# Sliding-window attention and a residual MLP: the same tasks in another written-out order

## The chip, the cores and the metric

The kernel runs on one core of a Trainium2 chip. Its time is the device time of one execution in microseconds (us). A profile is one further execution recorded by the hardware profiler; its span runs from the first to the last instruction of the core and is somewhat shorter than the time.

The core has these engines: TensorE (PE: matmuls and transposes; its weight loads are listed as PEld), VectorE (DVE), ScalarE (ACT), GpSimd (POOL) and SyncE (SP), which only issues transfers here. Transfers can be issued by SP and ACT (the profile's queue q1 is SP's, q10 is ACT's) and by GpSimd (queue q0, "software_dynamic"). Sixteen DMA engines carry all of them.

## The reference

Attention with a window of 128 keys and 4 sink keys, over 4 batches, 8 heads, 768 positions and 64 dimensions, and then a residual MLP with a mixing step over the positions. All inputs and the output are float32.

```python
def _attn_ref(q, k, v, n_sink, window):          # q, k, v: (4, 8, 768, 64)
    scores = scale * np.matmul(q, k.transpose(0, 1, 3, 2))
    keep = is_sink | in_window
    scores = np.where(keep, scores, -1000000000.0)
    a = softmax(scores)                          # written out in the original
    return np.matmul(a, v)

def _moe_ref(x, alpha1, beta1, w_tok, alpha2, beta2, w_ch1, w_ch2, lam):
    a1 = alpha1 * x + beta1                      # x: (4, 768, 512)
    tok = np.einsum('ts,bsd->btd', w_tok, a1)
    u = x + lam * tok
    a2 = alpha2 * u + beta2
    ch = np.maximum(a2 @ w_ch1, 0.0) @ w_ch2     # w_ch1: 512 x 2048
    return u + lam * ch
```

## The kernel before

**A list of tasks.** The kernel's body is written as 1143 tasks. Each is a Python function that issues one to some twenty instructions; it names the tasks whose results it needs and the buffers it uses. Nothing is issued while the tasks are collected. At the end one call writes them out by four tables of literals:

```python
plan.emit(ORDER, ENGINES, HOMES, IDLES)
```

ORDER is the sequence of task numbers in which the instructions are issued. Since each engine works off its instructions in the order in which they were issued, it fixes the stream of every engine and of every DMA queue. ENGINES gives for each task one digit: 0 ACT, 1 DVE, 2 TensorE, 3 GpSimd, 4 SP. HOMES says which slot of its kind each buffer takes (8 slots for q and k rows, `nat`; 4 for staged weights, `wst`; 2 for `hT`; and so on). IDLES lists filler matmuls on a tile `warm` of zeros (L148) that are put ahead of a task: `(73, 0, 65)` means 65 of them before task 73. The priorities and costs in the task functions play no part on the chip: there only true dependences of data and buffers, and the order of the queues, act.

**Stages.** Batch 0 starts with loads. `load_qk` (L397) brings q or k of a pair of heads (384 KB) through SP or ACT; for the later pairs of batch 0 (L390) GpSimd's queue brings them and converts to float16 on the way. `load_v0` (L424) brings v in blocks, `load_wtok` (L435) rows of w_tok. `trans` transposes q and k on TensorE (L507 for the pair that was cast on the core, L504 for those cast on the way), and the results are copied to `qkT` (L157). Then come the masked scores per block of 128 positions (bias and q k products, L612, L617, L678, L681), exponentials (L639, L686), the product with v (`pv`, L718), the division (L743, L744), and the multiplication with lam-alpha1 into `xh`, in halves of 256 columns on GpSimd in batch 0 (L753). `cast_wtok` casts and transposes w_tok (L809). `tok` (L849) is the mixing over positions, after which u is formed (L856) and cast (L155, L157).

For the channel MLP u is transposed (`uTp`, L890) and taken through the affine alpha2, beta2 (L873 on ACT). `mlp1` computes h for one block `fi` of 128 of the 2048 channels and 384 positions (four matmuls, L929), followed by a relu on ACT (L935) or DVE (L937). Block `fi` needs quarter `fi // 4` of w_ch1. The second product (L1046 and L1114) gives the result, which is added and stored (L1065, L1128). The batches follow each other; the attention of the next batch is woven into the MLP of the one before.

**Weights.** `load_w1` (L448) brings one quarter of w_ch1 (512 columns, 1 MB of float32 read) through GpSimd's queue, which converts it into the float16 tile `w1f`. `load_w2` (L444) brings pieces of w_ch2 into `wst`, from where `cast_w2` casts them. `lam_b` (L1235) is lam spread over the partitions.

**Gates.** A gate is a transfer of eight elements out of `w1f` through SP:

```python
def gate(i):
    add(-3000, {SP: 790}, lambda e: nc.sync.dma_start(
        gates[0:1, 8 * i : 8 * i + 8], w1f[0:1, 0, i * 512 : i * 512 + 8]), [done["w1", i]],
        lands=(1, 20))
```

It reads what quarter i writes, so SP waits there until that quarter has landed, and everything that stands behind it on SP's queue waits with it. There are gates for quarters 1, 2 and 3.

**The order before, around the change.** SP starts with row 0 of w_tok, q and k of pair 0, then v and the rest of w_tok, then a piece of w_ch2, lam, another piece of w_ch2, the gate of quarter 1, and only then loads for batch 1 and more of w_ch2, with the gates of 2 and 3 further on. GpSimd starts with k of pair 1, a small constant (`sel`), q of pair 1, another load, masks, another load, `bm`, and the identity `iden` (L326), which every transpose needs. After the first half of `xh` (L753) it issues the quarters 0, 1, 2, 3 of w_ch1 one after another, and then goes on with the halves. TensorE starts with 65 fillers, the transposes of w_tok 0 (L809), 12 fillers, the transposes of q and k of pair 0 (L507), those of k of pair 1 (L504), fillers, and scores. Its first h tasks are those of fi 1, 11, 8, 13, 12, 14; then come the `uTp` of the other half.

Of the kernel before, what the change touches and what calls it, by code (L numbers as in the profile page):

```python
# [77 lines left out]
def kernel(  # L78
# [119 lines left out]
    for r in range(NR):  # L198
# [18 lines left out]
        26, 6, 9, 7, 10, 5, 11, 8, 18, 15, 72, 19, 1, 12, 3, 0, 4, 2, 22, 14, 73, 74, 45, 48, 46,  # L217
        17, 39, 49, 47, 53, 13, 40, 50, 41, 90, 95, 43, 91, 51, 54, 103, 52, 16, 44, 61, 104, 42,
        96, 109, 100, 62, 107, 110, 63, 55, 28, 108, 92, 56, 101, 21, 68, 65, 59, 93, 20, 69, 97,
        102, 111, 94, 24, 98, 57, 60, 30, 112, 105, 23, 58, 99, 113, 128, 106, 114, 116, 25, 131,  # L220
        135, 78, 115, 64, 27, 138, 31, 32, 117, 132, 29, 129, 136, 33, 122, 66, 125, 34, 123, 137,
        119, 139, 126, 35, 79, 70, 120, 140, 124, 84, 71, 80, 133, 130, 141, 67, 146, 85, 134, 121,
        147, 144, 75, 118, 158, 86, 154, 148, 159, 145, 142, 87, 149, 150, 155, 160, 143, 76, 88,
        151, 156, 81, 77, 166, 152, 162, 167, 89, 127, 82, 163, 213, 83, 168, 209, 164, 165, 214,
        210, 153, 217, 179, 211, 178, 157, 197, 229, 36, 212, 215, 218, 185, 216, 226, 230, 219,
        176, 161, 177, 220, 169, 223, 222, 232, 225, 224, 221, 227, 237, 233, 279, 238, 234, 228,
        273, 280, 182, 171, 204, 291, 274, 175, 289, 292, 200, 231, 293, 290, 246, 294, 295, 199,
        384, 241, 248, 188, 186, 257, 296, 247, 172, 243, 277, 174, 181, 242, 259, 258, 187, 170,
        278, 267, 37, 260, 271, 358, 268, 198, 285, 349, 272, 381, 301, 286, 366, 351, 303, 302,
        189, 297, 378, 173, 304, 281, 180, 352, 203, 249, 190, 282, 298, 379, 250, 287, 380, 192,  # L230
        353, 385, 288, 206, 283, 386, 369, 375, 367, 265, 284, 368, 202, 370, 266, 363, 376, 371,
        253, 377, 201, 299, 254, 372, 364, 183, 382, 191, 300, 373, 615, 365, 275, 374, 383, 357,
        261, 276, 408, 262, 387, 263, 184, 409, 205, 195, 239, 411, 264, 410, 395, 269, 396, 240,
        397, 270, 196, 388, 614, 621, 235, 412, 400, 194, 244, 398, 236, 401, 255, 617, 251, 245,
        256, 389, 390, 399, 252, 311, 359, 207, 193, 391, 424, 616, 335, 425, 393, 341, 426, 392,
        336, 648, 427, 634, 413, 394, 312, 636, 414, 428, 419, 404, 420, 415, 360, 405, 313, 429,
        208, 422, 337, 416, 361, 441, 421, 622, 402, 314, 423, 442, 626, 403, 305, 638, 315, 406,
        430, 640, 316, 435, 431, 306, 641, 355, 436, 443, 619, 437, 338, 649, 618, 438, 362, 317,
        432, 637, 407, 307, 433, 345, 444, 339, 439, 635, 318, 445, 450, 434, 639, 644, 319, 451,
        628, 452, 620, 440, 308, 645, 340, 453, 417, 446, 323, 447, 418, 320, 309, 448, 324, 321,  # L240
        658, 322, 329, 449, 642, 659, 454, 325, 625, 643, 330, 646, 347, 455, 326, 623, 343, 647,
        464, 344, 456, 465, 348, 466, 460, 457, 467, 650, 327, 458, 331, 461, 629, 459, 472, 462,
        632, 463, 653, 356, 651, 656, 627, 332, 38, 654, 480, 333, 342, 624, 652, 473, 310, 476,
        468, 471, 470, 469, 481, 474, 488, 885, 477, 475, 482, 492, 655, 490, 493, 350, 483, 478,
        514, 491, 516, 489, 657, 479, 515, 660, 517, 630, 882, 665, 518, 663, 354, 328, 666, 502,
        880, 661, 664, 498, 879, 519, 508, 499, 346, 503, 678, 662, 512, 509, 679, 504, 513, 487,
        484, 671, 485, 676, 486, 506, 677, 877, 548, 505, 672, 680, 507, 526, 549, 546, 527, 631,
        334, 522, 674, 681, 528, 547, 907, 523, 534, 903, 529, 633, 682, 675, 878, 542, 683, 535,
        890, 689, 543, 550, 685, 684, 690, 510, 551, 494, 511, 673, 667, 544, 495, 668, 891, 496,
        686, 545, 901, 687, 669, 497, 693, 888, 688, 883, 530, 694, 670, 700, 531, 524, 897, 701,  # L250
        698, 500, 691, 525, 696, 699, 552, 501, 697, 704, 553, 558, 695, 705, 904, 692, 562, 559,
        706, 909, 887, 707, 563, 564, 898, 708, 702, 566, 565, 910, 715, 703, 567, 532, 716, 889,
        713, 533, 709, 714, 896, 520, 710, 556, 717, 521, 538, 557, 537, 540, 539, 536, 560, 541,
        899, 718, 921, 572, 922, 881, 711, 574, 884, 573, 576, 712, 561, 719, 902, 577, 575, 555,
        727, 720, 569, 908, 721, 580, 728, 578, 722, 581, 729, 554, 723, 905, 730, 568, 739, 724,
        579, 725, 592, 570, 911, 726, 582, 740, 593, 588, 912, 583, 595, 584, 571, 906, 743, 589,
        731, 585, 900, 590, 732, 605, 744, 587, 733, 596, 606, 734, 607, 611, 594, 597, 602, 745,
        612, 586, 613, 599, 895, 603, 591, 757, 765, 600, 758, 601, 759, 766, 741, 771, 760, 742,
        916, 772, 751, 917, 746, 773, 752, 913, 761, 919, 774, 886, 767, 918, 604, 762, 763, 598,
        768, 777, 764, 779, 920, 923, 780, 914, 755, 915, 778, 608, 756, 926, 930, 735, 609, 931,  # L260
        924, 927, 781, 736, 925, 775, 782, 737, 928, 753, 929, 893, 738, 934, 754, 892, 769, 935,
        932, 610, 941, 770, 819, 776, 942, 894, 939, 820, 821, 940, 937, 936, 823, 749, 822, 945,
        748, 824, 938, 747, 827, 933, 948, 950, 750, 952, 943, 951, 825, 953, 787, 828, 944, 807,
        788, 797, 826, 808, 949, 946, 829, 798, 801, 954, 830, 791, 802, 956, 947, 792, 783, 955,
        957, 963, 961, 784, 789, 958, 962, 811, 790, 964, 959, 785, 812, 965, 805, 786, 795, 806,
        960, 967, 796, 799, 793, 968, 966, 970, 972, 794, 813, 971, 969, 815, 973, 814, 809, 800,
        816, 803, 810, 974, 978, 804, 976, 979, 837, 975, 977, 835, 838, 980, 841, 836, 839, 842,
        818, 843, 840, 845, 981, 832, 982, 846, 817, 986, 844, 831, 990, 987, 983, 988, 847, 991,
        984, 851, 833, 992, 1002, 993, 834, 848, 855, 852, 985, 849, 1003, 859, 856, 1004, 989,
        1006, 850, 860, 1005, 853, 998, 1007, 1008, 868, 999, 857, 1009, 997, 865, 995, 858, 862,  # L270
# [35 lines left out]
    )  # L306
    IDLES = (
        (73, 0, 65), (46, 0, 12), (49, 1, 1), (90, 3, 10), (61, 3, 2), (109, 3, 3), (92, 3, 1),
        (166, 1, 4), (162, 0, 1),
    )  # L310
    W1_SINCE = 20000.0

# [1010 lines left out]
```

The softmax here doesn't subtract the row's maximum and nothing guards it: scores larger than these inputs give would overflow.

## Time and profile before

| what | value |
|---|---|
| time, median of 3 runs | 258.25 us (256.22 to 258.77) |
| span of the profiled execution | 254.3 us |
| mean granted TensorE clock | 0.997 |
| TensorE busy | 245.6 us (97%) |
| VectorE busy | 190.7 us (75%) |
| ScalarE busy | 133.2 us (52%) |
| GpSimd busy | 103.2 us (41%) |
| quarter of w_ch1, issue to landing | 9.6 / 15.4 / 20.2 us (min / median / max) |
| q or k through GpSimd's queue (L390) | 6.7 / 7.7 / 8.3 us |
| DMA moved | 38.79 MB, 153 GB/s over the span |

The profiled execution has no time of its own beside its span; the three timed runs lie 1.9 to 4.5 us above that span. Busy time counts an engine's instructions, fillers included. Where a row names what an engine waited for, it is the one of several things that came last by the profile.

### The profile page before, as it was taken

How to read it: one execution, taken by the hardware profiler on the slowest of the kernel's cores; microseconds unless marked ns; L12 is line 12 of the kernel's file. 1: busy time of each engine (PE TensorE's matmuls, PEld its weight loads, DVE VectorE, ACT ScalarE, POOL GpSimd, SP SyncE). 2: the span in 40 equal slices, each digit the busy share in tenths (PEclk: the TensorE clock that was granted, in tenths of full speed). 3: DMA queues.
4: the chain of work that ended last, by engine and by line, in shares of the span. 5: the costliest groups of instructions: out<-in, count | busy, mean ns of one | idle time of the engine just before them, and what ended most of it. 6: DMA issues, size and time to landing. Idle time of an engine off the chain costs nothing.

```text
span 254.3 us, 5499 instructions
## 1 busy us (share of the span) xinstructions
PE 245.6 (97%) x2167; PEld 159.9 (63%) x2167; DVE 190.7 (75%) x402; ACT 133.2 (52%) x219; POOL 103.2 (41%) x124
## 2 busy tenths in 40 slices
PE   7799997999999999999999999999999999999993
PEld 7554644666555544566687686667667676667882
DVE  5688986767888874978879995578778983228892
ACT  2599913879977034787833434566660235543000
POOL 8318845876455527515782040065662120000010
PEclk9999999999999999999999999999999999999998
DMA  6999999899999999998484764520000140100327
GB/s 182 205 215 266 272 269 316 246 377 300 221 158 233 234 208 156 195 249 180 110 170 107 128 122 138 144 65 0 3 0 3 30 84 13 41 0 3 117 73 268
DMA packets 86129, 38.79 MB, mean 153 GB/s; under 512 B 73540, under 2 KB 80460, under 8 KB 86104
## 3 DMA queue, kind: packets, MB, share of 16 engines
q1 hardware_dynamic: 66576, 28.06, 47.3%
q10 hardware_dynamic: 15784, 7.11, 11.8%
q0 software_dynamic: 3744, 3.28, 8.0%
q8 instruction: 17, 0.28, 0.4%
q14 instruction: 8, 0.07, 0.1%
HBM read 29.91 MB, written 6.29 MB: 142 GB/s over the span
## 4 chain that ended last, share of the span: by engine, by line
PE 84%; DMA 11%; DVE 2%; POOL 1%; SPq 0%; issue 0%
PE h L929 32%; PE P L1046 22%; PE tok L849 9%; PE ch L1114 8%; DMA w1f<-in_moe_w_ch_dram 8%; PE pv L718 3%; PE S L617 3%; DMA nat<-in_k_dram 3%; PE tp L507 1%; POOL w1f L448 1%; PE tp L504 1%; DVE qkT L157 1%; DVE E L696 1%; PE pv L711 1%; PE pv L604 1%; PE idle L148 0%
## 5 line engine op out<-in xcount | busy, mean ns | idle before, releaser
L929 PE MATMUL h<-uT,w1f 128*128 128x384 f16 x512 | 89.8, 326 | 1.5 <-DMA w1f<-in_moe_w_ch_dram 1.5
L929 PEld LDWEIGHTS <-w1f 128*128 128x128 f16 x512 | 48.2, 98 | 32.7 <-DMA w1f<-in_moe_w_ch_dram 1.9
L935 ACT ACTIVATE hT<-h 128x384 f16<-128x384 f32 x77 | 37.0, 491 | 39.5 <-PE h L929 39.3
L937 DVE TENSOR_SCALAR hT<-h 128x384 f16<-128x384 f32 x51 | 27.8, 555 | 23.4 <-PE h L929 22.8
L1046 PEld LDWEIGHTS <-hT 128*128 128x128 f16 x408 | 39.5, 98 | 6.7 <-issue 0.2
L639 ACT ACTIVATE E<-S 128x1024 f16<-128x1024 f32 (+1 forms) x39 | 38.1, 1001 | 7.6 <-PE S L617 6.3
L762 POOL TENSOR_TENSOR tm<-x,la_b 128x512 f32<-128x512 f32 x18 | 24.3, 1353 | 24.2 <-DVE x L744 12.3
L849 PE MATMUL tok<-xh,wtokT 128*128 128x512 f16 x144 | 33.0, 379 | 0.0
L1059 DVE TENSOR_TENSOR x<-x,P 128x256 f32<-128x256 f32 x45 | 18.3, 419 | 11.3 <-PE P L1046 10.2
L1046 PE MATMUL P<-w2f,hT 128*128 128x256 f16 x216 | 26.5, 273 | 0.0
L849 PEld LDWEIGHTS <-wtokT 128*128 128x128 f16 x144 | 13.9, 98 | 15.0
L1114 PE MATMUL ch<-w2f,hT 128*128 128x512 f16 x96 | 23.2, 379 | 0.0
L1046 PE MATMUL P<-w2s,hT 128*128 128x256 f16 x192 | 23.1, 273 | 0.0
L1082 POOL TENSOR_TENSOR x<-x,pt 128x256 f32<-128x256 f32 x4 | 3.4, 854 | 47.5 <-DVE pt L1077 47.5
L155 ACT CAST u<-x 128x512 f16<-128x512 f32 x15 | 9.2, 615 | 24.9 <-DVE x L856 24.3
L744 DVE TENSOR_TENSOR x<-pv,rec 128x256 f32<-128x256 f32 x48 | 20.4, 425 | 1.7
L155 ACT CAST n<-nat 128x768 f16<-128x768 f32 x21 | 16.9, 828 | 8.9 <-DVE x L1125 6.4
L718 PEld LDWEIGHTS <-E 128*128 128x128 f16 x328 | 14.8, 98 | 5.1 <-issue 1.1
L856 DVE TENSOR_TENSOR x<-x,tok 128x512 f32<-128x512 f32 x24 | 16.0, 683 | 2.3 <-PE tok L849 2.3
L718 PE MATMUL pv<-vfs,E 128*128 128x65 f16 x328 | 17.7, 194 | 0.0
L579 POOL TENSOR_SCALAR_AFFINE_SELECT E<-E 128x512 f16<-128x512 f16 x12 | 7.5, 648 | 20.6 <-ACT E L639 20.6
L743 DVE RECIPROCAL rec<-pv 128x4 f32<-128x4 f32 x48 | 8.6, 179 | 7.2 <-PE pv L718 6.9
(134 smaller groups left out, 340.6 us busy)
## 6 DMA issues: line engine op xcount, KB each, us to landing
wst_w<-in_moe_w_ch_dram SPq DMA_DIRECT2D x8, 512.0 KB, 8.2
nat<-in_q_dram SPq DMA_DIRECT2D x10, 384.0 KB, 3.9
vnat<-in_v_dram SPq DMA_DIRECT2D x14, 256.0 KB, 5.7
nat<-in_k_dram SPq DMA_DIRECT2D x8, 384.0 KB, 7.2
out_dram<-x SPq DMA_DIRECT2D x11, 256.0 KB, 3.1
out_dram<-x ACTq DMA_DIRECT2D x10, 256.0 KB, 3.7
wtn<-in_moe_w_tok_dram SPq DMA_DIRECT2D x6, 384.0 KB, 4.1
w1f<-in_moe_w_ch_dram POOLq DMA_DIRECT2D x4, 512.0 KB, 15.4
```

The costliest lines, as they stand in the source:

```text
L155: nc.scalar.copy(o, i)
L639: nc.scalar.activation(eT.t, pS.t[:, :, 0 : n * w].rearrange("p e (i w) -> p e i w", i=n), AF.Exp, scale=scale)
L718: nc.tensor.matmul(po.t[:, hl, :], eT.t[:, e_, off + i, c : c + P], vf[j][:, h, :], start=(r < 2 and n == 0), stop=(n == len(parts) - 1 an ...
L744: nc.vector.tensor_mul(bx.t[:, 4 * G : 4 * G + 4, :], po.t[:, :, 0:D], rec.t.to_broadcast([P, 4, D]))
L762: engine[e].tensor_mul(bt.t, bx.t.rearrange("p h d -> p (h d)"), la1_b)
L849: nc.tensor.matmul(pt.t, wtokT[:, si, ti * P : (ti + 1) * P], hs[si].t, start=(si == 0), stop=(si == NR - 1))
L929: nc.tensor.matmul(ph.t, w1f[:, c, fi * P : (fi + 1) * P], bu.t[:, c, chk * NTOK : (chk + 1) * NTOK], start=(c == 0), stop=(c == NC - 1))
L935: nc.scalar.activation(bh.t[:, fi, :], ph.t, AF.Relu)
L937: nc.vector.tensor_scalar_max(bh.t[:, fi, :], ph.t, 0.0)
L1046: nc.tensor.matmul(pc.t, hh[:, nt * P : (nt + 1) * P], w(fi), start=(first and n_ == 0), stop=(n_ == HF - 1), skip_group_check=True)
L1059: nc.vector.tensor_add(row(bx)[:, cols], row(bx)[:, cols], pc.t)
L1114: nc.tensor.matmul(pc.t, bh.t[:, fi, nt * P : (nt + 1) * P], w2f[:, fi, :], start=(fi == 0), stop=(fi == NF - 1))
```

## The change

The functions and the tasks are the same; the four tables ORDER, ENGINES, HOMES and IDLES are replaced. 182 tasks go to another engine. What differs in the order, in words:

- SP's front: k of pair 0, q of pair 0, then row 0 of w_tok, then v (before: row 0 of w_tok, q, k, v).
- GpSimd's front: k and q of pair 1, `bm`, `iden`, three more loads, then `sel`, masks, and the last load.
- TensorE's front: 65 fillers, transposes of q and k of pair 0, 17 fillers, transposes of q of pair 1, 3 fillers, scores, w_tok 0, 6 fillers, transposes of k of pair 1; 7 and 6 fillers further on. There are 104 fillers in all instead of 99.
- The quarters of w_ch1: 2 and 1 after two halves of `xh`; then three halves, a cast and another half; then 3; then six more halves; then 0. The first h tasks are fi 10, 5, 15, 12, 6, then two `uTp`, 8, and fi 1; two transposes of batch 1 stand ahead of the first.
- The gates stand behind all of SP's loads of batch 1 and w_ch2. Directly behind the last row of w_tok SP issues k and q of batch 1, lam, more k and q, a piece of w_ch2, a block of v, and another piece of w_ch2.
- ACT issues six loads for batch 1 and w_ch2 before the first h (k of pair 2, a piece of w_ch2, k of pair 0, then q of pair 0, another piece and q of pair 3 between its casts of u and an affine). 34 transfers are issued by ACT instead of 24, by SP 101 instead of 111.
- The multiplication of lb1 (L1164) goes from DVE to GpSimd, the first cast of w_tok from DVE to ACT; casts, relus and stores are dealt anew.

Cut from the diff (tasks 26, 6, 7: row 0 of w_tok, q, k; 32 to 35: quarters 0 to 3; 36 to 38: gates 1 to 3):

```diff
     ORDER = (
-        26, 6, 9, 7, 10, 5, 11, 8, 18, 15, 72, 19, 1, 12, 3, 0, 4, 2, 22, 14, 73, 74, 45, 48, 46,
...
-        135, 78, 115, 64, 27, 138, 31, 32, 117, 132, 29, 129, 136, 33, 122, 66, 125, 34, 123, 137,
-        119, 139, 126, 35, 79, 70, 120, 140, 124, 84, 71, 80, 133, 130, 141, 67, 146, 85, 134, 121,
...
-        210, 153, 217, 179, 211, 178, 157, 197, 229, 36, 212, 215, 218, 185, 216, 226, 230, 219,
...
-        278, 267, 37, 260, 271, 358, 268, 198, 285, 349, 272, 381, 301, 286, 366, 351, 303, 302,
...
-        632, 463, 653, 356, 651, 656, 627, 332, 38, 654, 480, 333, 342, 624, 652, 473, 310, 476,
...
+        7, 6, 9, 26, 8, 10, 11, 3, 0, 14, 48, 12, 15, 20, 45, 5, 46, 49, 1, 47, 17, 50, 51,
...
+        71, 34, 135, 129, 138, 33, 132, 42, 125, 115, 139, 117, 146, 140, 130, 147, 118,
+        136, 84, 141, 133, 67, 126, 137, 82, 148, 78, 142, 134, 35, 158, 149, 143, 150, 159,
...
+        157, 32, 214, 89, 165, 217, 169, 210, 215, 378, 229, 211, 216, 171, 218, 372, 212,
...
+        508, 487, 36, 675, 548, 509, 899, 522, 549, 348, 889, 494, 523, 887, 526, 495, 673,
...
+        999, 992, 983, 851, 834, 984, 986, 1000, 985, 856, 858, 847, 833, 38, 1002, 987,
...
+        1025, 1028, 37, 1010, 1017, 1022, 864, 1029, 1040, 1011, 1027, 1012, 1013, 1034,
...
     IDLES = (
-        (73, 0, 65), (46, 0, 12), (49, 1, 1), (90, 3, 10), (61, 3, 2), (109, 3, 3), (92, 3, 1),
-        (166, 1, 4), (162, 0, 1),
+        (46, 0, 65), (51, 2, 17), (95, 2, 3), (53, 2, 6), (92, 3, 7), (57, 0, 6),
     )
```

## The prediction

> **What bounds the kernel now.** I read the page's chain that ended last first, then the busy time by stretch, then every idle gap of TensorE, then what released the one large gap, and last what the DMA queues were doing at that moment.
>
> The chain's shares (the page, section 4), then the row of the granted clock:
>
> ```profile
> PE 84%; DMA 11%; DVE 2%; POOL 1%; SPq 0%; issue 0%
> ...
> PEclk9999999999999999999999999999999999999998
> ```
>
> TensorE (PE) is the chain for 84%, at full clock in every slice. The stretches (columns: TensorE, weight loads, VectorE, ScalarE, GpSimd busy, clock, DMA share, GB/s):
>
> ```profile
> 5.00:10.00 5.00, 3.19 (x51) 2.75 (x48) 2.12 (x6) 1.85 (x3) 3.19 (x10) 1.00 1.12 195
> ...
> 35.00:40.00 5.00, 5.00 (x35) 2.62 (x33) 4.97 (x9) 1.96 (x3) 1.67 (x2) 1.00 1.20 239
> 40.00:45.00 5.00, 3.50 (x22) 1.95 (x21) 2.07 (x5) 1.69 (x4) 3.85 (x4) 1.00 1.11 350
> 45.00:50.00 5.00, 5.00 (x41) 3.25 (x40) 4.53 (x8) 4.38 (x9) 4.10 (x4) 1.00 0.91 253
> ```
>
> From 45 to 250 us every stretch of this view shows TensorE full. What comes late before 45 is therefore never made up, and what comes early is kept unless a later wait eats it. There are two holes: about 1.8 us between 5 and 10, and 1.5 us between 40 and 45. The timeline of TensorE names both (start, us, what, idle before it and releaser):
>
> ```profile
> 1.06 5.04 PE L148 MATMUL idle<-warm 128*128 128x128 f16 x65 [1.06 <-DVE warm L174]
> 7.60 0.49 PE L809 MATMUL wT<-iden,wt 128*128 128x128 f16 x6 [1.50 <-POOL iden L326]
> ...
> 9.63 0.51 PE L507 MATMUL tp<-iden,n 128*128 128x128 f16 x6 [0.26 <-DVE n L157]
> 10.06 0.53 PE L504 MATMUL tp<-iden,n 128*64 128x128 f16 x12
> ...
> 39.83 2.11 PE L929 MATMUL h<-uT,w1f 128*128 128x384 f16 x12
> 43.45 2.12 PE L929 MATMUL h<-uT,w1f 128*128 128x384 f16 x12 [1.50 <-DMA w1f<-in_moe_w_ch_dram]
> ```
>
> The second hole is the fourth h task (x12 are three tasks of four matmuls) waiting for the last quarter of w_ch1. The chain in order of time, up to 46 us, shows why that came at 43.40: the four loads leave GpSimd in 21.0 to 24 us, and the last is 20 us on its way.
>
> ```profile
> 1.72 7.26 DMA nat<-in_k_dram
> ...
> 21.01 2.22 POOL w1f L448 x3
> 23.23 20.17 DMA w1f<-in_moe_w_ch_dram
> 43.45 2.12 PE h L929 x12
> ```
>
> So the price of the change is fixed by when the last needed quarter lands, and that by who shares the 16 DMA engines with it. The queue shares of 29.0 to 33.3 us, of 38 to 40 us (GpSimd's row alone) and the SyncE (SP) issues show it:
>
> ```profile
> q0 software_dynamic: 509, 0.51, 70.9%
> q1 hardware_dynamic: 325, 0.63, 43.9%
> ...
> q0 software_dynamic: 405, 0.41, 121.9%
> ...
> 27.00 0.43 SPq L444 DMA_DIRECT2D wst_w<-in_moe_w_ch_dram  x1
> 35.96 0.80 SPq L455 DMA_DIRECT2D gates<-w1f  x1
> 38.28 3.56 SPq L397 DMA_DIRECT2D nat<-in_k_dram  x1
> ```
>
> The shares always add to 1.13 to 1.22: the engines are full, and one queue's gain is another's loss. The gate at L455 waits for quarter 1 and stands from 27.4 to 35.96; all that time SP asks for nothing more, so GpSimd's queue (q0) has one rival (q1), for two microseconds none.
>
> **The change, part by part.** Tasks and arithmetic are the same: no matmul of the computation is added. What moves:
>
> *The gates.* The three gates go far back in SP's order, behind batch 1's q, k, v and w_ch2 loads. Directly behind the last w_tok row SP now asks for k hp1, lam, q hp1, k hp3, q hp2, a w_ch2 piece, a v block and another w_ch2 piece, with nothing to hold them. ScalarE (ACT), which issued two loads before 60 us (36.9 and 41.2), now issues k hp2 at about 28 (behind the last exp of the second head group), then a w_ch2 piece and k hp0, then three more between its casts of u: a third queue (q10) that is busy while w_ch1 travels.
>
> *The quarters.* Before: 0, 1, 2, 3 back to back. Now 2 and 1 about as early, 3 after three halves, a cast and another half, and 0 behind six more halves, at some 31 to 32 us (a half, L753, is 0.74). The order of h follows: fi 10 (quarter 2), 5 (1), 15 (3), 12, 6, two uTp, 8, and as seventh fi 1 (quarter 0). Since a queue serves its transfers one after another and quarter 2 holds it until 28.9, the late issue alone costs nothing; its cover is the three quarters ahead of it.
>
> *When the last quarter lands.* Work is counted as time of all 16 engines together. A quarter: 70.9% of 4.3 us, by 512 of 509 packets, is 3.07. Plain loads: 43.9% of 4.3 us for 0.63 MB is 3.0 us per MB; I take 2.9 with the neighbouring stretches: 384 KB is 1.15, 512 KB 1.55, lam 0.77, a v block of some 1.3 (many small packets). Up to 28.9 two rows are at work as before. Left then: GpSimd 3 x 3.07 = 9.2; SP 1.0 of w_tok + 4 x 1.15 + 0.77 + 2 x 1.55 + 1.3 = 10.8, less the 2.8 that q1 was served from 23.5 to 28.9 (50.8% of 5.5), = 8.0; ACT 4 x 1.15 + 2 x 1.55 = 7.7. Together 24.9 at 1.15 is 21.7 us: all done at 50.6, the last semaphore 0.5 later (packets ended 42.91, semaphore 43.40): **51.1**. Bounds: if GpSimd's queue keeps the share that it has against one rival, 43.4 as before; if it gets a strict third throughout, 8.0 a quarter, 28.9 + 24 + 0.5 = 53.4. I take 51.1: the total is what the full engines must serve, and three queues have work most of that time.
>
> [...]
>
> *What TensorE pays.* Before, the fourth h could have started at 39.83 + 2.11 = 41.95 and did at 43.45. In the new order three more h (3 x 0.65), two uTp (0.67) and two batch-1 transposes (0.68) stand ahead of the first task of quarter 0: the same progress is 43.45 + 3.3 = 46.75. Now it is 51.1: **+4.3 us**. The wait may split: quarter 3, evenly spaced, comes at 43.9, and the third h wants it nearly 2 us earlier; the sum is the same. Nothing behind it has slack, as the full stretches from 45 to 250 show.
>
> *The front.* k and q of the first pair come first, so they should land in the places that w_tok and q had (3.8 and 4.8) instead of k at 8.98; the identity needs only bm and two loads ahead of it on GpSimd. The first transposes then start right after the 65 fillers, at 6.1. But the third (q of hp 1) waits for GpSimd's second load, 10.66 before, issued one row (0.72) sooner: 10.0, and scores and w_tok's transposes stand behind it. At 10.56 before, w_tok 0 (0.33) and the transposes of k hp1 (0.46) were already done, and 21 fillers were still to come, where it is 22 now (0.067 each): lateness 10.0 - 10.56 + 0.33 + 0.46 + 0.07 = +0.3. Bounds: load at 8.05, where TensorE is through with its 17 fillers: -1.65; at 10.66: +0.96. As long as w_ch1 is the later, this is worth nothing in the sum: TensorE reaches quarter 0's first task at 41.95 + 3.3 + 0.3 = 45.55 and waits 5.5.
>
> *The rest.* 182 tasks change engine (relus, casts, stores dealt between SP and ACT, one 1.35-us multiply of lb1 from VectorE to GpSimd, which is busy 1.8 of the 10 us from 10 to 20): no TensorE wait in the rows from 46 to 250 depends on them; counted as nothing, with bounds of -0.5 (there are few waits to win) and +1.5 (one more wait of the second hole's size). The tail's order is the same, 4.2 us from the last matmul to the end.
>
> *Sum.* 254.3 + 4.3 = 258.6 of span. The runs shown lie 1.9 to 4.5 above this span, the median 3.9: 258.25 + 4.3 = **262.6**. The case's own range, with landing between 49.3 and 53.4 and the rest's bounds, is 260.3 to 266.4 (258.25 + 2.55 - 0.5 and 258.25 + 6.65 + 1.5).
>
> [...] The granted clock stays 1.00 through the 1.5-us wait. [...]
>
> **Rivals.** About 1% is what a measurement of this kernel tells from no change.
>
> (1) *No longer wait.* GpSimd's queue keeps its two-row pace, for which its 509 packets to 325 speak, and the last quarter is in by 45.5: the 1.5 goes, the front's 0.3 comes: 257.05. Landings up to 49.3 end within 1% too. Against it: the busy third queue, and no gate. Chance 0.26.
>
> (2) *Faster, the other side.* As (1), and the front's gain survives: GpSimd's second load is in by 8.05, since w_tok no longer rides ahead of it: 258.25 - 1.5 - 1.65 = 255.1. It decides only if the last quarter lands by about 43.6 as well (45.25 - 1.65). Against it: six such loads took 6.7 to 8.3 each before. Chance 0.08.
>
> (3) *Worse.* ScalarE's three issues stand ahead of an affine (L873) that the first h needs. The k issue of 38.28 above took 3.56 where its neighbours took 0.4: an issue can stand until an older transfer is through. Three such are 10.7, less the 3.0 that ScalarE has free from 35 to 40: first h at 40.8 + 7.7 = 48.5, quarter 0's first task six h and two uTp later (4.6) at 53.1: 6.4 behind 46.75, 264.6. It decides from the point where more than 5.5 us are lost there. Chance 0.11.
>
> My forecast has the remaining 0.55.
>
> **How the numbers follow.** Time: the likeliest, 262.6. Range 256.5 to 266.5: up to the dearest of the forecast and (3) with a little of the unsized rest, down to (1) with its half microsecond of the rest; (2) and some of (3)'s top stay outside. Faster by over 1%: 0.08 (case 2); within 1%: 0.26 (case 1); slower: 0.55 + 0.11 = 0.66.
>
> **What would show it.** Right: TensorE waits some 5 us in all for w1f ahead of the first seven h, ended near 51 by quarter 0, 18 to 20 us after its issue; q10 busy from 29 to 49; the gates issued late without a wait; the first transposes at 6.1 and a wait of L504 until about 10 for GpSimd's load; stretches full from 52 on, the end 4 later. Wrong: under 1.5 us of wait for w1f, or TensorE idle elsewhere, above all behind ScalarE's issues.

## The result, and the profile after

The changed kernel takes 273.1 us (median; 272.4 to 273.9) against 258.5 us of the kernel before in the same measurement: a ratio of 1.061 (95% interval 1.054 to 1.068). The forecast was 262.6, with a range of 256.5 to 266.5: the sign was right, the size was not. Ratios compare the faster executions alone, without those more than 1.5% above the fastest of their kernel; medians and ranges are of all. The profiled span went from 254.3 to 271.8 us, 17.5 longer; that is more than the medians differ, since each execution's own span lies 1.7 to 2.4 us below its time, so that the span of 254.3 belongs to an execution of some 256 to 257 us and not to one of 258.25, which the prediction's sum started from. Line numbers are four higher than before, since the tables are longer.

The page's chain shares and its row of the granted clock, after:

```profile
PE 64%; DMA 16%; DVE 8%; POOL 3%; SPq 3%; issue 2%; ACT 2%; ACTq 0%; DVEq 0%; POOLq 0%
...
PEclk9979999999999996899999999999999999999999
```

TensorE is on the chain for 64% instead of 84%, and its clock falls twice, near 17 and near 107 us. The stretches (length, TensorE, weight loads, VectorE, ScalarE, GpSimd busy, clock, DMA share, GB/s):

```profile
10.00:15.00 5.00, 2.90 (x47) 1.90 (x47) 1.56 (x2) 2.36 (x5) 0.00 (x0) 1.00 1.26 200
15.00:20.00 5.00, 4.39 (x41) 2.23 (x42) 4.06 (x11) 1.89 (x4) 2.00 (x3) 0.66 0.88 203
...
40.00:45.00 5.00, 3.89 (x27) 1.91 (x26) 3.54 (x7) 2.54 (x4) 1.36 (x2) 1.00 1.16 265
...
50.00:55.00 5.00, 3.10 (x27) 1.87 (x26) 2.77 (x7) 1.65 (x3) 3.75 (x4) 1.00 0.93 327
...
100.00:150.00 50.00, 43.09 (x342) 24.63 (x341) 30.57 (x61) 29.60 (x50) 25.80 (x30) 0.93 0.73 149
```

The last row is the surprise: now 6.9 us of TensorE are missing and the mean clock is 0.93, where TensorE was full before:

```profile
100.00:150.00 50.00, 50.00 (x431) 33.08 (x430) 43.31 (x89) 31.95 (x51) 20.94 (x22) 1.00 0.81 159
```

TensorE's timeline gives each gap its releaser:

```profile
10.54 0.53 PE L508 MATMUL tp<-iden,n 128*64 128x128 f16 x12 [1.68 <-DMA n<-in_q_dram]
15.61 0.34 PE L572 MATMUL vsp<-vfs,sel 128*128 128x256 f16 x1 [2.17 <-DVE vfs L157]
...
48.08 2.12 PE L933 MATMUL h<-uT,w1f 128*128 128x384 f16 x12 [0.63 <-DMA w1f<-in_moe_w_ch_dram]
...
53.60 2.12 PE L933 MATMUL h<-uT,w1f 128*128 128x384 f16 x12 [1.56 <-DMA w1f<-in_moe_w_ch_dram]
...
105.90 0.82 PE L621 MATMUL S<-qkT 64*128 64x256 f16 x6 [5.85 <-DMA qkT<-n]
```

So there are three places. Up to the first task of quarter 0 (46.75 by the prediction's count before, 53.60 now) the kernel lost 6.85 us: at the front and at w_ch1. At 100 us it lost 5.85 of waiting and, by the rows of single microseconds, the clock was at half from 106 to 111, which is another 2.7 us of TensorE's work. The remaining 2 us or so are gaps of 0.3 to 0.7 and pieces that I did not follow further.

The third place, at SP. Its timeline before, and then after (start, us, what):

```profile
78.63 12.98 SPq L523 DMA_TRANSPOSE qkT<-n  x7
92.13 0.69 SPq L407 DMA_DIRECT2D vnat<-in_v_dram  x1
92.94 2.27 SPq L523 DMA_TRANSPOSE qkT<-n  x1
```

```profile
84.87 6.25 SPq L527 DMA_TRANSPOSE qkT<-n  x4
91.18 0.58 SPq L405 DMA_DIRECT2D nat<-in_k_dram  x1
91.85 4.84 SPq L527 DMA_TRANSPOSE qkT<-n  x3
96.74 0.57 SPq L405 DMA_DIRECT2D nat<-in_q_dram  x1
97.41 5.76 SPq L527 DMA_TRANSPOSE qkT<-n  x1
```

The q and k of batches 2 and 3 are not transposed on TensorE: eight transfers of SP do it (the last branch of `trans`). They may start only when batch 1's scores have read the single buffer qkT, so they begin 6.2 us later, by the lateness inherited from the first two places. From their start TensorE comes to batch 2's scores after 20.2 us before, without a wait, and after 15.2 us now (100.05, where the wait of 5.85 begins). Its row before:

```profile
98.86 0.61 PE L617 MATMUL S<-qkT 64*128 64x256 f16 x8
```

In the new ORDER these scores stand ahead of four tok tasks instead of behind them. The last transpose lands at 105.85, 21.0 us after the start.

### The profile page after: what moved, and what is told of

Same layout as the page of the kernel before. It is cut to its first block, busy times and chain, and to the rows that moved or that the text cites. A ratio compares the mean times of both kernels' runs of the same rounds, so it can differ in the third digit from the quotient of the medians.

```text
span 271.8 us, 5532 instructions
## 1 busy us (share of the span) xinstructions
PE 252.0 (93%) x2172; PEld 161.8 (60%) x2172; DVE 199.5 (73%) x406; ACT 123.7 (46%) x204; POOL 114.5 (42%) x136
## 4 chain that ended last, share of the span: by engine, by line
PE 64%; DMA 16%; DVE 8%; POOL 3%; SPq 3%; issue 2%; ACT 2%; ACTq 0%; DVEq 0%; POOLq 0%
PE h L933 25%; PE P L1050 19%; PE tok L853 8%; DMA w1f<-in_moe_w_ch_dram 6%; DMA v<-in_v_dram 4%; DMA qkT<-n 3%; PE pv L722 3%; PE S L621 3%; SPq L527 3%; POOL xh L757 2%; PE ch L1118 2%; DMA uT<-u 1%; DVE x L748 1%; DMA nat<-in_k_dram 1%; DVE uT L879 1%
## 5 line engine op out<-in xcount | busy, mean ns | idle before, releaser
L939 ACT ACTIVATE hT<-h 128x384 f16<-128x384 f32 x79 | 37.4, 491 | 41.6 <-PE h L933 41.0
L766 POOL TENSOR_TENSOR tm<-x,la_b 128x512 f32<-128x512 f32 x18 | 24.5, 1362 | 41.6 <-DVE x L748 14.7
L941 DVE TENSOR_SCALAR hT<-h 128x384 f16<-128x384 f32 x49 | 26.6, 553 | 19.0 <-PE h L933 18.1
L853 PE MATMUL tok<-xh,wtokT 128*128 128x512 f16 x144 | 34.5, 391 | 0.0
L1118 PE MATMUL ch<-w2f,hT 128*128 128x512 f16 x96 | 24.1, 390 | 0.0
L1089 POOL TENSOR_TENSOR x<-x,pt 128x512 f32<-128x512 f32 x1 | 1.3, 1267 | 41.8 <-issue 41.8
L155 ACT CAST n<-nat 128x768 f16<-128x768 f32 x12 | 10.0, 831 | 19.6 <-DMA nat<-in_k_dram 10.2
L157 POOL CAST u<-x 128x512 f16<-128x512 f32 x9 | 5.5, 611 | 30.9 <-DVE x L860 26.9
L621 PE MATMUL S<-qkT 64*128 64x256 f16 (+1 forms) x156 | 13.0, 276 | 5.8 <-DMA qkT<-n 5.8
L722 PEld LDWEIGHTS <-E 128*128 128x128 f16 x328 | 14.6, 97 | 5.3 <-issue 1.8
L722 PE MATMUL pv<-vfs,E 128*128 128x65 f16 x328 | 17.1, 194 | 0.3 <-ACT hT L939 0.3
```

Source lines behind the costliest of these rows:

```text
L155: nc.scalar.copy(o, i)
L621: nc.tensor.matmul(pv_[:, e_, i, :], o.t[rows, 2 * hp + 1, j * P : (j + 1) * P], o.t[rows, 2 * hp, j * P : j * P + w], start=not bias, sto ...
L722: nc.tensor.matmul(po.t[:, hl, :], eT.t[:, e_, off + i, c : c + P], vf[j][:, h, :], start=(r < 2 and n == 0), stop=(n == len(parts) - 1 an ...
L766: engine[e].tensor_mul(bt.t, bx.t.rearrange("p h d -> p (h d)"), la1_b)
L853: nc.tensor.matmul(pt.t, wtokT[:, si, ti * P : (ti + 1) * P], hs[si].t, start=(si == 0), stop=(si == NR - 1))
L939: nc.scalar.activation(bh.t[:, fi, :], ph.t, AF.Relu)
```

## The experiments

Each is a kernel of its own: the kernel before, or the changed one, with the tables edited. Diffs are in task numbers. The line numbers of those built on the changed kernel are those of the kernel before; in numbers 6, 7, 8 and 12 they are one higher.

**1. The late load.** q and k of pair 1 of batch 2 share a slot in the changed kernel (616 and 617, slot 2), which is why the second is asked for at 91.18.

```diff
-ORDER: ... 615, 404 ... 639, 308 ... 450, 617, 324, 451, 645 ...    nat slot of 617: 2
+ORDER: ... 615, 617, 404 ... 639, 308 ... 450, 324, 451, 645 ...    nat slot of 617: 7
```

> The changed kernel with one edit: the load of k of pair 1 of batch 2 (task 617) gets a slot of its own among the q and k slots (7 instead of 2, where q of the same pair still sits) and is asked for by SP directly behind its neighbour at about 77.5 us, not at 91.2 behind four transposes. Theory: the 5.85-us wait of TensorE at 100 us and the half clock after it (together some 9 us) come from this late load, which alone holds back the last transposed block of qkT. Then the wait for qkT goes to under 2 us and the time falls from 273.1 by 6 to 9, to 264 to 267. Rival: the last transpose is held by the load of batch 3 that stands directly ahead of it on SP's queue (asked for at 96.7, 8.4 us on its way); then the landing stays near 105 and the time within 1.5 us of 273.

Measured: 270.7 us (268.4 to 272.0), ratio 1.050 (1.042 to 1.059); TensorE still waits 4.09 for qkT, which lands at 104.89. The cast of that load is now done by 90.5 on ScalarE, and the last transpose still lands 14 us later: the late load was not what held it. ScalarE's next row:

```profile
104.99 0.83 ACT L155 CAST n<-nat 128x768 f16<-128x768 f32 x1 [14.51 <-DMA qkT<-n]
```

The late load is worth about 1 us of landing (1.8 counted from the first transpose, at 85.67 here: 19.2 us instead of 21.0), not the loss. And ScalarE stands 14.5 us before its next cast, which needs the slot of the very transpose that is late; I saw what that meant only in number 5.

**2. The load of batch 3 in the way.**

```diff
-ORDER: ... 318, 883, 882, 448, 641, 330 ...
+ORDER: ... 318, 882, 448, 641, 883, 330 ...
```

> The changed kernel with one edit: SP's load of q of pair 3 of batch 3 (task 883) goes behind the last transpose of batch 2 instead of directly ahead of it. Theory of the late load: the cast of k of pair 1 is done only at 96.6, so the last transpose still can't start before 96.7; it lands 2.9 us after (the least a transpose took) to 5 us after, at 99.6 to 102, and TensorE's wait falls from 5.85 to between 0 and 2, the time to 264 to 269 as well: here both are needed for the loss. If the transfers of ScalarE asked for at 95.8 and 96.2 are what the transpose queues behind, nothing changes: 272 to 274.

Measured: 271.6 (269.2 to 273.0), ratio 1.055 (1.045 to 1.064), wait 4.25, landing 104.35. Again 1.5 us of landing. Neither neighbour alone holds the transpose (both edits together were not run); the eight together take some 20 us in both kernels, with the DMA engines at a share of 1.29 to 1.30 from 80 to 98 us before, and of 1.31 to 1.36 from 90 to 105 after.

**3. Fillers into the wait.**

```diff
+IDLES: (658, 0, 60)
```

> The changed kernel with 60 fillers of 0.067 us (4.0 us) added on TensorE ahead of the sink row of batch 2, at about 98.6 us, so that TensorE works through most of its wait for qkT. Nothing else moves. If the loss at 100 us is the wait alone, the time stays at 273.1 within 0.7 us, or grows. If the half clock from 104.3 to 111.1 us costs as much as it looks (some 3 us), the granted clock stays near 1.00 there and the time falls by 2 to 3.5 us, to 269.6 to 271, although TensorE has more to do.

Measured: 270.1 (269.6 to 272.9), ratio 1.051 (1.044 to 1.059). In the profile the wait fell to 1.73, yet the clock still went to a half from 105 to 109, and a wait of 1.22 for uT came in at 119.7; the span fell by 0.9 only. But that is the execution that took 272.9 us, at a mean clock of 0.987. The other three took 269.6 to 270.4 at a mean clock of 0.992 to 1.00, where the four of the changed kernel have 0.969 to 0.981. So with the clock kept the kernel is some 3 us faster, as forecast, though TensorE has 4 us more to do. How much of that belongs to 100 us and how much to the half clock at the front these executions do not show.

**4. The front.** In the changed kernel the cast of the first two v blocks (63) stands on VectorE ahead of the copy of k of pair 1, and the sink row matmul that needs it (68) ahead of scores. The v blocks land later than before, behind row 0 of w_tok.

```diff
-ORDER: ... 53, 63, 19, 103, 54, 68, 104, 22, 100, 92, 105, 74, 93, 21, 4, 101, 106 ...    63 on DVE
+ORDER: ... 53, 19, 103, 54, 104, 22, 100, 92, 105, 63, 74, 93, 21, 4, 101, 68, 106 ...    63 on POOL
```

> The changed kernel with its front mended in one place: the cast of the first two v blocks (task 63) on GpSimd as in the kernel before, not on VectorE ahead of the copy of k of pair 1, and the sink row matmul that needs it (task 68) behind the sinks' matmul, not ahead of the scores. Theory: TensorE's 2.17-us wait at 13.4 us goes, and the half clock from 15.7 to 19 with it: TensorE is 3 to 3.8 us earlier at 25 us, the first load of w_ch1 leaves earlier by 2 to 3.5, and the wait for qkT at 100 us keeps its size: 269 to 271. Rival: the wait for w_ch1 eats it, because the transfers set its landing and not the time of its issue: 272 to 273.5.

Measured: 271.6 (270.8 to 272.5), ratio 1.055 (1.050 to 1.060). The 2.17-us wait is gone and the first load of w_ch1 leaves at 23.73 instead of 25.64. A half clock stays, from 10.6 to 14.0, behind a wait of 2.47 that ends at 10.51. What arrives at the first task of quarter 0 is 1.4 us: it starts at 52.21, after waits of 2.38 for the affine and 1.21 for w1f. Neither the theory's time nor the rival's is met, and the 1.4 us are not firm: numbers 10 and 13, the same code up to there, differ by 2.4 at this place. By their ratios numbers 1 to 4 are 0.6 to 1.1% below the changed kernel, with intervals that overlap its own.

**5. The scores alone.**

```diff
-ORDER: 653 ... 654 ... 655 ... 656 ... 480 (tok 5)
+ORDER: ... 480, 653, 654, 655, 656
```

> The changed kernel with one edit: TensorE's first scores of batch 2 (task 653, and the exponentials that follow from it) go behind four tok tasks of batch 1 (2, 0, 1, 5: 24 matmuls of 0.38, 9.1 us of work) instead of ahead of them, much as in the kernel before. New theory after the runs so far: the eight transposes into qkT need some 20 us from their start in either kernel (78.6 to 98.1 before, 84.9 to 105.9 now); what changed is that TensorE asks for qkT only 15.2 us after that start instead of 20.2. Then the wait of 5.85 and the half clock after it go and the time falls by 7 to 9, to 264 to 266. Rival: the work that was moved in front only hides the wait, and the tasks of batch 2 that come later (sinks, exponentials) make TensorE wait again at once: 269 to 272.

Measured: 273.2 (273.0 to 275.2), ratio 1.065 (1.057 to 1.073): nothing gained. TensorE's wait has only moved, and ScalarE's timeline says why:

```profile
107.80 2.72 PE L849 MATMUL tok<-xh,wtokT 128*128 128x512 f16 x6 [3.62 <-DVE x L856]
...
113.50 0.40 PE L549 MATMUL sk<-qkT,ks 128*32 128x512 f16 x4 [2.22 <-DVE x L856]
```

```profile
105.26 0.83 ACT L155 CAST n<-nat 128x768 f16<-128x768 f32 x1 [8.55 <-DMA qkT<-n]
```

And VectorE's timeline:

```profile
106.13 0.42 DVE L961 TENSOR_TENSOR w2s<-w2f 128x512 f16<-128x512 f16 x1 [3.81 <-ACT n L155]
```

That cast is task 903, k of pair 1 of *batch 3*. It stands ahead of batch 2's scores on ScalarE, and needs the slot of the last transpose of batch 2. While ScalarE waits for it, VectorE waits for a slot that the cast frees, the additions for tok stand behind VectorE's wait, and tok's PSUM slots stay taken. A second engine asked for the late transfer, in a place that no row of TensorE's timeline names.

**6. The scores ahead, in the kernel before.**

```diff
-ORDER: ... 647, 464 (tok 2) ... 653 ...
+ORDER: ... 647, 653, 656, 654, 464 (tok 2) ...
```

> The kernel before with one edit, the counterpart: the first scores of batch 2 go ahead of the tok tasks, directly behind the last of the batch's transposes in the list. Theory: TensorE asks for qkT at about 92.7 and gets it at 98.1: a wait of 5.4, and a half clock after it (some 2.7): slower by 7 to 9, 265 to 267. Rival (the lateness of the changed kernel at 100 us is inherited from its later transfers, not made by TensorE's order): slower by less than 3.

Measured: 265.7 (264.0 to 268.9), ratio 1.032 (1.022 to 1.041): some 8 us, as the theory had it. TensorE's waits at the third place:

```profile
101.42 0.40 PE L618 MATMUL S<-qkT 64*128 64x256 f16 x2 [2.91 <-DMA qkT<-n]
103.55 0.40 PE L618 MATMUL S<-qkT 64*128 64x256 f16 x2 [1.74 <-DMA qkT<-n]
```

It asked at 98.5, 14.6 us after the first transpose (83.92), and the clock was at half from 101 to 108: together some 7 us, by an estimate from these numbers. This one move, six microseconds earlier in TensorE's order, shows a price of that size at the third place in the other kernel. It is not free of lateness, though: the profile is of the execution that took 268.9 us, in which TensorE already stood 2.37 us at 32.11, with half the clock from 33 to 40, and the transposes began 5.3 us later than in the kernel before. The other three (264.0 to 266.4) have no profile.

**7. No gates, in the kernel before.**

```diff
-ORDER: ... 197, 229, 36, 212 ... 278, 267, 37, 260 ... 616 ...
+ORDER: ... 197, 229, 212 ... 278, 267, 260 ... 616, 36, 37 ...
```

> The kernel before with one part of the change alone: the gates of the quarters 1 and 2 go behind SP's loads for batch 1 and the first ones of batch 2, so that nothing holds these loads back while w_ch1 travels. Theory: the last quarter, without rivals for part of its way before, shares the queues throughout and lands 3 to 5 us later than 43.4; the wait of 1.5 grows to 4.5 to 6.5 and the time by 3 to 5, to 261 to 263.5. Rival: SP's loads are through before they matter, or GpSimd's queue keeps its share: within 1 us of before.

Measured: 262.2 (259.8 to 262.7), ratio 1.018 (1.010 to 1.027); the profiled span grows by 3.5, in the execution that took 259.8 us. TensorE's two waits:

```profile
42.17 1.47 PE L930 MATMUL h<-uT,w1f 128*128 128x384 f16 x8 [1.09 <-DMA w1f<-in_moe_w_ch_dram]
46.97 2.12 PE L930 MATMUL h<-uT,w1f 128*128 128x384 f16 x12 [3.32 <-DMA w1f<-in_moe_w_ch_dram]
```

The last quarter lands 3.5 us later (46.92 instead of 43.40). This is the prediction's mechanism by itself, at 3.5 us in this profile and at 4.7 by the ratio, where it was given 4.3.

**8. w_ch1 early, in the kernel before.**

```diff
-ORDER: ... 115 ... 27, 138, 31, 32, 117 ... 136, 33, 122 ... 125, 34, 123 ... 126, 35, 79 ...
+ORDER: ... 32, 33, 34, 35, 115 ... 27, 138, 31, 117 ... 136, 122 ... 125, 123 ... 126, 79 ...
```

> The kernel before with the four quarters of w_ch1 asked for ahead of the first half of xh on GpSimd, at 16 to 18 us instead of 21 to 24. Theory (the landing follows from the bytes ahead and beside it, and the row is free then): the last quarter lands by 41, the wait of 1.5 goes, 256 to 257.5. Rival: the v and w_tok loads that attention needs lose their turns to it, and TensorE waits between 17 and 35 us for what it did not wait for before: 258 to 261.

Measured: 266.0 (265.1 to 267.2), ratio 1.035 (1.027 to 1.043). The last quarter lands at 38.41, five microseconds early, and the loads that attention needs pay for it: TensorE waits 1.84 and 2.19 for w_tok's chain and then 5.56, up to 37.92, for a division (L745) that stands on VectorE behind the cast of a late v block; the clock is at half from 31 to 42. Neither forecast had so much.

```profile
36.37 0.96 DVE L157 CAST vfs<-v 128x768 f16<-128x768 f32 x1 [8.94 <-DMA v<-in_v_dram]
```

**9. Scores and cast together.** To number 5 comes: 903 behind the sinks' exponential (652), its load 880 in slot 7; the scores are the same four tasks behind tok 5.

```diff
-ORDER: ... 624, 631, 903, 455, 653, 650 ... 652, 472 ...     nat slot of 880: 1
+ORDER: ... 624, 631, 455, 650 ... 652, 903, 472 ...          nat slot of 880: 7
```

> The changed kernel with two edits. As in the earlier run, TensorE's first scores of batch 2 go behind four tok tasks. And ScalarE's cast of k of pair 1 of batch 3 (task 903), which waits for the slot of the last transpose of batch 2 and held ScalarE from 96.7 to 105.3 us with the casts of u and the copies for tok behind it, goes behind the sinks' exponential of batch 2; its load gets slot 7, so that nothing else waits for it. Theory: the loss at 100 us needs both, an early demand on TensorE and an early demand on ScalarE; with both gone TensorE works through: no wait over 1 us between 95 and 115, clock 1.00, time 264 to 266.5. Rival: the region is bound by what VectorE and ScalarE do for tok, whatever the order: 269 to 273.

Measured: 266.5 (264.7 to 267.9), ratio 1.033 (1.023 to 1.043): 6.6 us less than the changed kernel. One wait over a microsecond is left there, 2.76 at 105.7, and the clock is at 0.66 from 110 to 115.

**10. The front added** (the edits of 4 and 9).

> The same with the mended front of the earlier run as well (cast of the first v blocks on GpSimd, the sink row matmul behind the sinks'). That alone brought 1.4 us at the wait for w_ch1 and 1.3 us at 105 us. Theory: it adds up, as there is nothing left behind it that waits for a transfer: 1 to 2 us less than the run before, 262.5 to 265. Rival: swallowed at the transposes of batch 2 or 3: the same time as the run before within 0.7.

Measured: 267.4 (266.3 to 268.4), ratio 1.038 (1.030 to 1.046), span 264.9 against 265.9. No gain in the times. TensorE comes to the first h earlier and stands 3.25 us for the affine; it starts quarter 0 at 51.51, 4.8 after the 46.75 that the prediction counts for the kernel before. TensorE's timeline, and then ScalarE's:

```profile
45.79 0.51 PE L507 MATMUL tp<-iden,n 128*128 128x128 f16 x6 [3.25 <-DVE uT L875]
```

```profile
44.16 0.67 ACT L873 ACTIVATE uT<-uTp,ab 128x384 f16<-128x384 f16 x1 [4.04 <-DMA wst_w<-in_moe_w_ch_dram]
```

The affine waits for a piece of w_ch2 that it does not use: between them in ScalarE's order stands the issue of q of pair 3, which left at 43.74, when the older piece had landed. This is the prediction's third rival. The changed kernel's own profile does not show it; those of numbers 1, 4 and 9 do, with waits of 2.19, 2.38 and 1.71.

**11. A gate put back** (number 10, and the following).

```diff
+ORDER: 173, ... 175, 36, ...    ENGINES: 175, 192, 171, 170, 191, 176 on SP instead of ACT
```

> The same with the gate of quarter 1 back on SP's queue, behind the two k loads that the first transposes of batch 1 need, and with the six loads that ScalarE issues before the first h put on SP at the same places of the list, so that they stand behind the gate. Theory: in the kernel before, taking the gates away cost 3.5 us at w_ch1; putting one back brings as much here, less what TensorE then waits for other things: quarters 3 and 0 land 3 us or more earlier, no wait for w_ch1 over 0.5, 2 to 3.5 us less than the run before: 259.5 to 262.5. Rival: the held loads come too late for the transposes of batch 1 at 55 to 60 us or for w_ch2, and TensorE waits there: not faster than the run before.

Measured: 269.1 (267.3 to 271.7), ratio 1.043 (1.031 to 1.055). Quarter 0 lands at 42.28, 9 us earlier, and it helps nothing: GpSimd stands in a cast (366) of a load that is now held, ahead of the last cast of u.

```profile
53.33 1.46 PE L890 MATMUL uTp<-iden,u 128*128 128x128 f16 x12 [7.39 <-POOL u L157]
```

**12. k and q first, in the kernel before.**

```diff
-ORDER: 26, 6, 9, 7, 10, 5 ...  IDLES: (73, 0, 65), (46, 0, 12), (49, 1, 1)
+ORDER: 7, 6, 26, 9, 8, 10, 3, 0 ... 46 ... 49 ... 53, 72, 73 ...  IDLES: (46, 0, 65), (53, 3, 13)
```

> The kernel before with the front of the change alone, without its early sink row: SP asks for k and q of pair 0 ahead of row 0 of w_tok; GpSimd makes the identity directly behind two loads; TensorE goes from the 65 fillers to the transposes of q and k of pair 0, 13 fillers, k of pair 1, then w_tok 0, and on as before. Theory: the hole of 1.5 us at 6.1 shrinks and the third transposes come at about 9.3 instead of 10.06: 0.5 to 1 us gained by 20 us, all swallowed by the wait for w_ch1 at 43.4, which grows from 1.5 to 2 or 2.5: within 0.8 us of before. Rival: w_tok's row or the v blocks land later by the same amount and TensorE waits between 10 and 25 us: slower by 1 to 3.

Measured: 258.1 (255.6 to 264.8), ratio 1.002 (0.997 to 1.007). The same, but not by the expected road: in the profile the clock was at a half from 11 to 17 us, behind waits at the front (1.18 and 0.79, and 0.89 in the half clock itself), and TensorE, later at w_ch1, found its last quarter landed (at 42.36). The hole of 1.5 swallowed a loss there, not a gain. This depends on the execution: four of the ten have a mean clock of 0.998 to 1.00 and took 255.6 to 256.8 us, the profiled one has 0.987 and took 258.3.

**13. The mask moved too** (number 10, with 655 behind tok 5's addition (481) and 650 behind the cast of u (466)).

> The run with scores, cast and front mended, and with two more moves at 100 us: VectorE's mask of the first scores of batch 2 goes behind the additions of the tok tasks, and ScalarE's copies of the sink keys behind its cast of the first u. Theory: the last wait of 2.9 us near 107 and the half clock after it come from VectorE and ScalarE standing in order behind what needs qkT; without them TensorE has no wait over 1 us between 95 and 115 and the run is 3 to 4.5 us faster than the one without these moves (267.4, span 264.9): 262.5 to 264.5, span near 261. Rival: TensorE gets to the h tasks of batch 1 earlier and waits there for uT's transposes, which come no earlier: less than 1.5 us.

Measured: 267.7 (266.1 to 269.1), ratio 1.042 (1.034 to 1.051), span 264.6. The wait of 2.9 became one of 1.54 and the clock stayed at 1.00 from 100 to 115, which speaks for the same early demand as the remainder there; the time doesn't show it, in part because this profile reached w_ch1 2.4 us later than that of number 10 (53.87 against 51.51) with the same code up to there. 7.1 of its 10.3 us over the kernel before are lost by then.

**14. Gate and casts** (number 13 and the gate of number 11, with casts 366 and 195 later).

> The same with the gate of quarter 1 back on SP, ScalarE's six early loads on SP behind it, and the two casts that would stand in the way of TensorE while their loads are held (k of pair 0 of batch 1 on GpSimd, a piece of w_ch2 on VectorE) put behind others. Theory: w_ch1 lands near 42 as in the earlier run with a gate, TensorE waits neither for it nor for u, and gains 3 to 5 us over the run before: 258 to 261, about the kernel before. Rival: the transposes of batch 1 at 55 us or the casts of w_ch2 wait for the held loads: no gain.

Measured: 267.1 (265.9 to 269.9), ratio 1.041 (1.034 to 1.048). Quarter 0 lands at 43.05, much as the last quarter of the kernel before (43.40), TensorE waits neither for it nor for u, and stands 3.02 us for the next cast on GpSimd, with the clock at a half from 52 to 58.

```profile
52.55 0.82 PE L507 MATMUL tp<-iden,n 128*128 128x128 f16 x6 [3.02 <-POOL n L157]
```

**15. Only w_ch2 and v held** (number 13; the gate ahead of w_ch2's pieces and v but behind the q and k loads of batch 1, ScalarE's two w_ch2 pieces on SP, its last load behind the affine).

```diff
+ORDER: ... 174, 36, ... 185, 192, 191, 205 ... 224, 176 ...    ENGINES: 192, 191 on SP instead of ACT
```

> The run with all mends at 100 us and at the front, and with less beside w_ch1 than the changed kernel has, but not the q and k loads: the gate of quarter 1 goes on SP behind the four q and k loads of batch 1 and ahead of the w_ch2 pieces and v blocks; ScalarE's two w_ch2 pieces go to SP behind it; ScalarE's load of q of pair 3 goes behind the affine that the first h needs (task 224), and VectorE's first cast of w_ch2 behind a relu. Theory: some 9 us of transfer work (three or four pieces of 1.55, a v block of 1.3) leave the time before w_ch1 has landed, so quarter 0 lands 3 to 5 us earlier than 51.5 to 53.9, and the wait of 3.3 behind the affine goes: the span falls from 264.6 to 260 to 262, the time to 262.5 to 265. Rival: the casts of q and k on GpSimd and ScalarE, which stand ahead of u's, are what TensorE waits for, whatever lands when: less than 1 us gained, 266.5 to 268.

Measured: 268.1 (266.1 to 269.7), ratio 1.048 (1.042 to 1.053): the rival. Quarter 0 lands at 46.79 and TensorE waits for no w1f; it waits for a cast of u that stands behind another of ScalarE's issues, and later for a copy of qkT, and comes to quarter 0 near 51.5 as in number 10.

```profile
42.02 0.28 PE L890 MATMUL uTp<-iden,u 128*128 128x128 f16 x2 [2.22 <-ACT u L155]
```

None of these beats the kernel before. Numbers 9, 10, 13, 14 and 15 all lie between 266.5 and 268.1, by their ratios 3.3 to 4.8% above it, though between them each named wait went away. That the landing of w_ch1 is not what holds 14 and 15 there is shown (43.1 and 46.8); that it is the order of casts, issues and loads on ScalarE and GpSimd is where the rows point, and no run with another such order was made.

## Why the prediction was wrong

*The bound, and "nothing behind it has slack".* TensorE is the bound, and what was late at w_ch1 stayed late. But from the full stretches I concluded that behind 46 us nothing could be lost either, and costed "the rest" at nothing with 1.5 at most. That term is the main failure: the place at 100 us cost 8.5 us in the profile, some 8 us in the kernel before by one move (number 6), and mending it gave back 6.6 (number 9). A full stretch of before says that its waits end in time, not by how much: the transposes must have been through by 98.86, when TensorE took them up without a wait, some 20 us after they started. I compared the order of h and the front task by task, and not the place of the scores, the slots of q and k, or the casts of the next batch.

*w_ch1.* The mechanism held: a third queue, no gate, waits at quarters 3 and 0, the last ended by quarter 0 17 us after its issue. But the waits are 2.2 us in all (0.63 and 1.56) where I had some 5, since TensorE came late itself. The terms were mis-sized in both directions. The quarters came 6.8, 5.1 and 5.5 us apart; I had 7.2 (24.9 us of work at 1.15) where the two-queue bound was 4.7. The queue shares of 44 to 50 us, after:

```profile
q0 software_dynamic: 658, 0.65, 63.5%
q10 hardware_dynamic: 457, 0.68, 30.0%
q1 hardware_dynamic: 707, 0.21, 23.2%
```

GpSimd's queue kept over half of the served time of this stretch (63.5 of 117%) against two rivals, with 658 of 1822 packets. The last quarter in the chain in order of time, after:

```profile
36.78 16.77 DMA w1f<-in_moe_w_ch_dram
```

That the bound by a strict third, 53.4, is met by 53.55 confirms nothing: the start was 4.7 us later (25.64 instead of 20.96). That start was in no term; I had let the first quarter's packets end at 28.9 as before, and they ended at 34.4 (landings by semaphore: 30.5 before, 36.1 after).

The shares of the kernel before also add less evenly than I wrote (1.13 to 1.22): to 1.24 from 38 to 40 us, and to 1.06 from 40.5 to 42.5:

```profile
q1 hardware_dynamic: 246, 0.45, 59.3%
q10 hardware_dynamic: 202, 0.31, 41.0%
q0 software_dynamic: 20, 0.02, 5.5%
```

There GpSimd's queue moved 20 packets in 2 us, and its last quarter still landed only at 43.40. The end of this quarter did not follow the shares of the queues; what held its last packets the trace does not tell.

*The front.* k and q landed at 3.84 and 5.00 and their transposes ran at 7.1 (forecast 6.1), and the wait for GpSimd's second load ended at 10.5 (forecast 10.0). Missed was the next wait, 2.17 at the sink row: the v blocks stand behind row 0 of w_tok now and landed at 15.0, and their cast was on VectorE, ahead of a copy that scores need. From the chain in order of time, after:

```profile
3.85 11.16 DMA v<-in_v_dram
15.04 0.44 DVE vfs L157
```

I had "lateness +0.3"; with the half clock it was nearer 4 when the first tok began, of which 1.4 passed through w_ch1 (number 4, by one profile).

*The clock.* The sum has no term for it: in the kernel before it had stayed at 1.00 through the waits of 1.5. In the profile after it cost 1.7 us from 15.7 to 19.1 and 2.7 at 106 to 111; the executions of number 3 that kept the clock were some 3 us faster.

*Rivals.* Rival (3), ScalarE's issues ahead of an affine, cost little in the changed kernel, where they took 0.4 to 0.5 each at 41.6 to 43.5. With an earlier front it was there, at 3.25 (number 10) of the 7.7 that I had given it, and smaller in numbers 1, 4 and 9. Rivals (1) and (2) fell with w_ch1's landing.

## What to carry to other kernels

Where an order is replaced wholesale, list for every late transfer all the engines that ask for it, with the time between its start and its first use in both orders; the first use may be a cast that only wants the transfer's buffer. A stretch in which the bound engine is full shows no margin, so cost "the rest" by its margins and not by its waits. Once several engines' orders have been written for one timing of the transfers, mending one of them only moves the wait: numbers 5, 10, 11, 14 and 15 each removed a wait that the profile named, and the time stayed.

## What the runs showed of the hardware

The granted clock fell behind some of TensorE's waits and stayed at 1.00 behind others. Single microseconds after, at the front and at 100 us (same columns as above):

```profile
16.00:17.00 1.00, 1.00 (x10) 0.58 (x9) 0.85 (x4) 0.00 (x0) 0.00 (x0) 0.50 0.39 89
...
106.00:107.00 1.00, 1.00 (x7) 0.31 (x6) 0.00 (x0) 0.99 (x3) 0.00 (x0) 0.50 0.29 47
```

At the front a wait of 2.17 us was followed by half the clock for 3.4 us (15.7 to 19.1), and at 100 us it was at half for 6.8 us (104.4 to 111.2), from within the wait of 5.85. In number 12 waits of 1.18 and 0.79, ended at 9.0 and 10.3, were followed by half of it from 10.6; a third wait, of 0.89, fell into that stretch, which lasted 6.8 us. In number 8 half the clock began at 31.4, behind a wait of 2.19 that ended at 30.5, and lasted some 10 us; a wait of 5.56 fell into it.

A wait of 3.25 us in number 10 left the clock at 1.00, and one of 2.91 in the same profile was followed by half of it for 3.4 us. Waits of 3.32 in number 7 (ended at 46.97) and of 3.35 in number 13 (at 47.59) left it at 1.00 too; shorter ones, of 1.73 in number 3 (at 105.20) and of 2.22 in number 15 (at 42.02), went with half of it for 3.4 us. In these profiles the length of one wait alone does not decide; what does they do not show.
